# One kernel for window attention and a four-expert attention layer: on-chip places given out by a table, two raw weights kept in one tile, and a new issue order

## The chip, the core and the metric

The kernel runs on one core of a Trainium2 chip. The core has five engines with an instruction queue each: TensorE (PE in the profile: matrix products and transposes), VectorE (DVE), ScalarE (ACT), GpSimd (POOL) and SyncE (SP, which here only issues transfers; ScalarE issues a few as well). Inputs and outputs lie in HBM, operands in SBUF (128 partitions), and results of TensorE in PSUM, which has eight banks of 2 KB per partition. The metric is the time of one execution on the device in microseconds, lower is better; the time of a kernel is the median of its runs.

## The reference, cut to what matters

Eight batches with eight heads of 64 columns and 576 positions. Stage 1 is attention in which a query sees itself and the 63 keys before it. Its result x goes through stage 2, a full causal attention for each of four experts, of which each position uses the two with the largest gate logits.

```python
def _attn_ref(q, k, v):                       # q, k, v: (8, 8, 576, 64)
    scores = scale * np.matmul(q, k.transpose(0, 1, 3, 2))
    mask = (rel >= 0) & (rel < window)        # rel = query - key, window = 64
    attn = softmax(np.where(mask, scores, -1e9))
    return np.matmul(attn, v)
def _moe_ref(x, w_gate, wq, wk, wv, wo):      # x: (8, 576, 512), 4 experts of 64 columns
    logits = x @ w_gate                       # the two largest give the weights w
    for e in range(E):
        q, k, v = x @ wq[e], x @ wk[e], x @ wv[e]
        a = softmax(np.where(causal, -1e9, scale * (q @ k.transpose(0, 2, 1))))
        ye = a @ v @ wo[e]
        out += w[..., e] * ye                 # where e is one of the position's two
    return out
```

## The kernel before, in words

**Two stages on one core.** Two heads form a pair and lie side by side on the 128 partitions; a batch has four pairs (`NP`). Stage 1 is cut into 36 units, each of eight tiles of 64 queries for two heads. Unit u goes through these steps, and the names are those of the rows below: `s1_qk(u)` computes 16 products of queries and keys into two PSUM banks (`s<-k,q`; the fourth pair's inputs lie in a buffer called `st`); ScalarE and VectorE bring them to SBUF as `sm` (VectorE by COPY_PREDICATED, which takes the own block of keys under the mask `own`); VectorE reduces maxima and sums (TENSOR_REDUCE, RECIPROCAL), GpSimd subtracts and scales, ScalarE takes the exponential; `s1_t(u)` transposes `sm` on TensorE (`t<-ident,sm`), ScalarE copies the result into `ft`, and VectorE (for the first nine units) or GpSimd makes the masked `pt` of it; `s1_av(u)` multiplies by the values (`o<-pt,v`). The result x is kept as a high part `xh` and the remainder `xl`.

**Stage 2** takes x with weights that are also split into two parts each (`wkhi`, `wklo`, and so on for q, v, o), so that each product is three matmuls (`three`). `split_weights(i)` does the split: ScalarE copies the raw weight into the high part, VectorE computes the low part by one SCALAR_TENSOR_TENSOR. The weight `wv` carries the four gate columns as well: 260 columns per chunk, of which 256 come from the tensor wv and four from w_gate, by two loads, two copies and two subtractions. Products: `v2ps` (values and gate logits, 12 matmuls for 128 positions), `kps` and `qps` (keys and queries), scores `s<-kt,qt`, softmax (VectorE's `p<-s,causal`, ScalarE's exponential, GpSimd's scaling), transposes of the probabilities by VectorE and transfers, `o<-pt,v` with the expert values, and `ops`, the output product, which is copied to `out` and stored by SP (the very last store by ScalarE).

**Order.** The class `Plan` records every instruction in a list in place of issuing it; a TensorE block (`nc.block`) is one entry. `Plan.issue` then issues the entries in the order of a table of numbers, `LIST` (2769 entries before). So the order on each engine's queue is that table, and semaphores make up the rest. All instructions have the line of the call in `issue`: L203 in the kernel before, L216 after. `warm(k)` is a block of products of `ident` with itself, whose result nobody reads.

**Places.** All PSUM tiles have the tag "s" with `bufs=8`: eight banks given out in rotation in the order in which the code allocates. In SBUF, `sm` rotates over three places of 2 KB, `ft` has one, `out` two (in the last batch some of `out` are in the places of `sm`). A tile that takes a place waits until the last reader of the tile before it is done; for an `out` that reader is the store.

Of the kernel before, what the change touches and what calls it, by code (L numbers as in the profile page):

```python
# [165 lines left out]
)  # L166
TAIL = 2
WARM = 6
BPOS = 0.05
SJOIN = 1  # L170
PARTS = ((0, 5), (5, 9))
# [47 lines left out]
def window_attention_moe_attention(ctx: ExitStack, tc: tile.TileContext, qT, kT, vW,  # L219
# [209 lines left out]
    def s1_av(u):  # L429
# [3 lines left out]
        with nc.block("a"):  # L433
            for i, (x, j, p, b) in enumerate(tiles(u)):
# [5 lines left out]
                if b == BLK - 1 and later(p):  # L440
                    freed.append(p)
# [527 lines left out]
```

## Time and profile before

| | |
|---|---|
| median of three runs | 412.88 us (412.17, 412.88, 413.45) |
| the profiled execution: own time, span | 413.24 us, 411.5 us |
| TensorE busy | 398.9 us, 97% of the span |
| VectorE busy | 310.7 us, 75% |
| GpSimd busy | 276.7 us, 67% |
| ScalarE busy | 260.5 us, 63% |
| chain that ended last | TensorE 87%, VectorE 8%, GpSimd 2% of the span |

The span runs from the first to the last instruction that the profiler saw; the execution's own time has 1.7 us around it. Busy shares are means over the whole span, and a stretch of some microseconds can look quite different from them. Times in rows are microseconds from the start of the span. In a row of the timeline the second number is how long the group lasts, from the start of its first to the end of its last instruction; instructions on VectorE and TensorE overlap a little, so start to start is what the queue takes.

### The profile page before, as it was taken

To read this page: it belongs to the slowest core of one execution; us is meant where nothing else is said; L and a number is where in the kernel's file an instruction comes from. 1 tells how busy PE (TensorE), PEld (TensorE's weight loads), DVE (VectorE), ACT (ScalarE), POOL (GpSimd) and SP (SyncE) were. 2 spreads that over 40 slices of the span, in tenths; PEclk is the share of its full clock that TensorE was granted. 3 is DMA by queue.
4 is the path that set the end of the run, shared out by engine and by line. 5 is a ranking of instruction groups with operands and counts; after the bars stand their busy time and mean duration, and the time that the engine had idled before them with its cause. 6 is when DMAs were issued, how large, how long until landed. Compare 5 with 4: busy or idle time off the path is not lost.

```text
span 411.5 us, 14007 instructions
## 1 busy us (share of the span) xinstructions
PE 398.9 (97%) x5308; PEld 358.9 (87%) x5308; DVE 310.7 (75%) x996; ACT 260.5 (63%) x865; POOL 276.7 (67%) x471
## 2 busy tenths in 40 slices
PE   7689999999999999999999999999999999999996
PEld 7479889999988989898989898988988999898875
DVE  3799998889695878879786876969887768445742
ACT  2666657685748485674858567486856676447852
POOL 3868887977797876887786966877768671504420
PEclk9899999999999999999999999999999999999999
DMA  7987346376867475368776669487657613453113
GB/s 240 349 310 268 111 144 231 78 208 181 239 223 203 135 182 217 106 172 267 193 248 143 205 147 308 130 211 197 176 130 222 151 60 80 131 134 103 53 53 127
DMA packets 33363, 72.69 MB, mean 177 GB/s; under 512 B 6160, under 2 KB 10256, under 8 KB 33296
## 3 DMA queue, kind: packets, MB, share of 16 engines
q1 hardware_dynamic: 32640, 71.14, 58.2%
q8 instruction: 42, 0.69, 0.7%
q10 hardware_dynamic: 656, 0.66, 0.5%
q14 instruction: 25, 0.20, 0.2%
HBM read 39.85 MB, written 9.44 MB: 120 GB/s over the span
## 4 chain that ended last, share of the span: by engine, by line
PE 87%; DVE 8%; POOL 2%; ACT 1%; issue 1%; ACTq 0%; POOLq 0%
PE o L203 18%; PE s L203 17%; PE ops L203 12%; PE v2ps L203 12%; PE kps L203 12%; PE qps L203 11%; PE t L203 4%; DVE pt L203 2%; DVE st L203 2%; DVE sm L203 1%; POOL sm L203 1%; PE warm L203 1%; DVE xl L203 1%; ACT sm L203 0%; DVE wklo L203 0%
## 5 line engine op out<-in xcount | busy, mean ns | idle before, releaser
L203 POOL TENSOR_SCALAR p<-p,r,g 128x448 f32<-128x448 f32 (+4 forms) x135 | 84.0, 636 | 29.5 <-DVE r L203 23.8
L203 POOL TENSOR_TENSOR sm<-sm,st 128x512 f32<-128x512 f32 x72 | 76.9, 1070 | 30.1 <-DVE st L203 20.0
L203 POOL TENSOR_SCALAR_AFFINE_SELECT pt<-ft 64x512 f32<-64x512 f32 x126 | 84.2, 668 | 17.5 <-ACT ft L203 8.4
L203 ACT ACTIVATE p<-p,r 128x192 f32<-128x192 f32 (+3 forms) x135 | 78.7, 588 | 16.9 <-DVE r L203 16.7
L203 PE MATMUL o<-pt,v 128*64 128x64 f32 (+2 forms) x1776 | 80.8, 249 | 1.8 <-DVE pt L203 1.2
L203 PEld LDWEIGHTS o<-pt,v 128*64 128x64 f32 x1776 | 68.2, 138 | 15.0 <-issue 3.2
L203 DVE STREAM_TRANSPOSE st<-p 128x128 f32<-128x128 f32 (+5 forms) x126 | 59.9, 515 | 5.7 <-POOL p L203 5.5
L203 DVE CUSTOM_DVE_ANT_0 p<-s,causal 128x320 f32<-128x320 f32 (+2 forms) x120 | 54.3, 483 | 7.8 <-PE s L203 7.3
L203 DVE TENSOR_REDUCE st<-sm 128x8 f32<-128x512 f32 x72 | 48.4, 679 | 7.0 <-ACT sm L203 6.1
L203 PE MATMUL s<-kt,qt 64*128 64x320 f32 (+3 forms) x480 | 43.3, 318 | 0.0
L203 DVE COPY_PREDICATED sm<-own,s 128x256 f32<-128x256 uint8 x72 | 29.3, 442 | 12.9 <-ACT sm L203 7.7
L203 PE MATMUL kps<-xh,wklo 128*128 128x256 f32 (+1 forms) x128 | 37.7, 295 | 1.2 <-DVE wklo L203 1.2
L203 PE MATMUL kps<-xh,wkhi 128*128 128x256 f32 (+1 forms) x128 | 38.7, 302 | 0.0
L203 PE MATMUL qps<-xh,wqhi 128*128 128x320 f32 (+1 forms) x128 | 38.4, 300 | 0.0
L203 PE MATMUL v2ps<-wvhi,xh 128*128 128x260 f32 x128 | 37.7, 294 | 0.2 <-DVE xl L203 0.2
L203 PE MATMUL s<-k,q 64*64 64x128 f32 (+1 forms) x1116 | 37.8, 275 | 0.1
L203 PE MATMUL qps<-xl,wqhi 128*128 128x320 f32 (+1 forms) x128 | 37.6, 294 | 0.0
L203 PE MATMUL kps<-xl,wkhi 128*128 128x256 f32 (+1 forms) x128 | 37.6, 294 | 0.0
L203 PE MATMUL qps<-xh,wqlo 128*128 128x320 f32 (+1 forms) x128 | 37.6, 294 | 0.0
L203 PEld LDWEIGHTS s<-kt,qt 64*128 64x128 f32 x480 | 35.0, 186 | 2.8 <-issue 0.7
L203 PE MATMUL v2ps<-wvhi,xl 128*128 128x260 f32 x128 | 36.2, 283 | 0.0
L203 PE MATMUL v2ps<-wvlo,xh 128*128 128x260 f32 x128 | 36.2, 283 | 0.0
(124 smaller groups left out, 921.6 us busy)
## 6 DMA issues: line engine op xcount, KB each, us to landing
v<-in_vW_dram SPq DMA_DIRECT2D x28, 576.0 KB, 5.2
pt<-st SPq DMA_DIRECT2D x112, 116.0 KB, 2.3
pt<-st SPq DMA_DIRECT2D x112, 80.0 KB, 2.1
out_dram<-out SPq DMA_DIRECT2D x32, 256.0 KB, 2.5
k<-in_kT_dram SPq DMA_DIRECT2D x28, 288.0 KB, 5.0
q<-in_qT_dram SPq DMA_DIRECT2D x28, 288.0 KB, 5.2
v<-in_vW_dram SPq DMA_DIRECT2D x3, 320.0 KB, 5.9
out_dram<-out SPq DMA_DIRECT2D x7, 128.0 KB, 2.5
```

Source lines behind the costliest of these rows:

```text
L203: call(*args, **kw)
```

## The change

1. The order table `LIST` is another one (2787 entries).
2. PSUM: eight tags of one bank each in place of the rotation; a string of 502 digits, `BANKS`, says which bank each tile takes, in the order of allocation.
3. SBUF: `sm`, `ft` and `out` share seven places of 2 KB (six before); a string of 108 digits, `SLOTS`, says which place each takes.
4. The raw wv and the raw gate weights go into one tile of four rows of 260 columns: the load of wv writes pieces of 256 columns, the load of w_gate pieces of four columns, and `split_weights` does one copy and one subtraction of 128x1040 in place of two of each.
5. `warm` is one matmul and there are 16 of them (six of two before).
6. `s1_qk` and `s1_av` of the units 0 to 3 are one block per pair in place of one per unit, so that the table can place them apart.
7. The `ops` bank is always allocated in full.

```diff
 LIST = (
-    1, 3, 2, 0, 7, 5, 6, 4, 16, 20, 18, 14, 15, 17, 9, 21, 19, 69, 29, 279, 46, 67, 48, 34, 35, 41, 44, 39, 42, 45,
...
+BANKS = (
+    "6737251201400112015230245536711342361037417672062047276356434472370430716515051730015260454245214522"
...
+SLOTS = (
+    "1601445624340310615206524305161165564345202460254161303524524520624136403622425165300534456123641053"
...
-WARM = 6
+WARM = 16
...
-    psum = ctx.enter_context(tc.tile_pool(name="psum", bufs=2, space=PSUM))
+    psum = ctx.enter_context(tc.tile_pool(name="psum", bufs=1, space=PSUM))
+    numbers = iter(BANKS)
+
+    places = iter(SLOTS)
+
+    def bank(shape, name):
+        return psum.tile(shape, F32, tag="s" + next(numbers, "0"), name=name)
+
+    def slot2k(shape, name):
+        return work.tile(shape, F32, tag="slot" + next(places, "0"), bufs=1, name=name)
...
-        t = (PT2[:, 0:1024], PT2[:, 1040:2064], PT2[:, 2064:3088], V2[1].rearrange("r j e c -> r (j e c)"))[i]
+        t = (PT2[:, 0:1040], PT2[:, 1040:2064], PT2[:, 2064:3088], V2[1].rearrange("r j e c -> r (j e c)"))[i]
         name, src, n, _ = WEIGHTS[i]
-        raw = raws[name] = t[:, :1024].rearrange("r (c n) -> r c n", n=src.shape[2])
-        nc.sync.dma_start(raw, src)
+        w = src.shape[2]
+        raw = raws[name] = t[:, :n].rearrange("r (c n) -> r c n", c=src.shape[1])
+        nc.sync.dma_start(raw[:, :, 0:w], src)
         if name == "v":
-            raws["g"] = PT2[:, 3088:3104].rearrange("r (c n) -> r c n", c=4)
-            nc.sync.dma_start(raws["g"], wg)
+            nc.sync.dma_start(raw[:, :, w:], wg)
...
-        at = 0
-        for raw in (raws.pop(x) for x in (name, "g")[:1 + int(name == "v")]):
-            to = slice(at, at + raw.shape[2])
-            nc.scalar.activation(hi[:, :, to], raw, AF.Copy, scale=scale)
-            nc.vector.scalar_tensor_tensor(lo[:, :, to], raw, scale, hi[:, :, to], op0=OP.mult, op1=OP.subtract)
-            at = raw.shape[2]
+        raw = raws.pop(name)
+        nc.scalar.activation(hi, raw, AF.Copy, scale=scale)
+        nc.vector.scalar_tensor_tensor(lo, raw, scale, hi, op0=OP.mult, op1=OP.subtract)
...
+    def parts(u):
+        t = list(tiles(u))
+        return [[x for x in t if x[2] == p] for p in sorted({x[2] for x in t})] if u < 4 else [t]
...
-        banks = [psum.tile([128, 4, 128], F32, tag="s", bufs=8, name=f"s1_{u}_{x}") for x in range(2)]
-        with nc.block("s"):
-            for x, j, p, b in tiles(u):
+        banks = [bank([128, 4, 128], f"s1_{u}_{x}") for x in range(2)]
+        for group in parts(u):
+            with nc.block("s"):
+                for x, j, p, b in group:
...
-        sm = work.tile([128, 512], F32, tag="sm1", bufs=3, name=f"sm1_{u}")
+        sm = slot2k([128, 512], f"sm1_{u}")
...
-        f = work.tile([128, 4, 128], F32, tag="ft", bufs=1, name=f"ft_{u}")[:, :m]
+        f = slot2k([128, 4, 128], f"ft_{u}")[:, :m]
...
         with nc.block("z"):
-            for i in range(2):
-                nc.tensor.matmul(ps[:, 0:128], lhsT=ident, rhs=ident, start=True, stop=True)
+            nc.tensor.matmul(ps[:, 0:128], lhsT=ident, rhs=ident, start=True, stop=True)
...
-        tag, bufs = ("out", 2) if b < NB - 1 or j % 2 else ("sm1", 3)
-        t = work.tile([128, DM], F32, tag=tag, bufs=bufs, name=f"out_{b}_{j}")
+        t = slot2k([128, DM], f"out_{b}_{j}")
```

The order is shown at three places. Numbers behind a name tell tiles apart, and they differ between the two kernels.

The first place is the beginning of SP's queue, the loads. Before, the first rows are:

```order
L203 DMA q_75<-in_qT_dram 128x256
L203 DMA q_73<-in_qT_dram 128x256
L203 DMA st_69<-in_qT_dram 128x256
L203 DMA q_77<-in_qT_dram 128x256
L203 DMA q_75<-in_qT_dram 128x320
L203 DMA st_69<-in_qT_dram 128x320
```

After the change they are:

```order
L216 DMA pt_70<-in_wv_dram 128x4x256
L216 DMA q_75<-in_qT_dram 128x256
L216 DMA q_73<-in_qT_dram 128x256
L216 DMA st_69<-in_qT_dram 128x256
L216 DMA q_75<-in_qT_dram 128x320
L216 DMA q_77<-in_qT_dram 128x256
```

The load of wv has moved from row 16 to row 1, and the first half of the third pair's queries (q_77) from row 4 to row 6. The first halves of the keys are on ScalarE's queue in both kernels. Each load signals on one of eight counters in turn, so the load in row 6 first waits for the load of the counter's row before, which ScalarE's four loads included is wv's.

The second place is the beginning of TensorE's queue. Before:

```order
L203 MATMUL warm_102<-ident 128x128 x2
L203 MATMUL warm_105<-ident 128x128 x2
L203 MATMUL warm_100<-ident 128x128 x2
L203 MATMUL warm_103<-ident 128x128 x2
L203 MATMUL s_0_0_106<-k_74,q_73 64x64 x2
L203 MATMUL s_0_1_107<-k_74,q_73 64x128 x2
```

After the change the queue begins with the scores of unit 0, and from row 31 on, when those of the units 0 to 3 are nearly done, it reads:

```order
L216 MATMUL s_3_0_143<-k_78,q_77 64x128 x2
L216 MATMUL warm_106<-ident 128x128
L216 MATMUL s_3_1_144<-st_69 64x128 x2
L216 MATMUL warm_108<-ident 128x128
L216 MATMUL warm_107<-ident 128x128
L216 MATMUL warm_102<-ident 128x128
L216 MATMUL warm_110<-ident 128x128
L216 MATMUL t_0_122<-ident,sm_0_118 128x128 x4
```

Eight dummies stood ahead of the first scores and none does now; the scores of the units 2 and 3 stand ahead of the first transposes, where before only those of unit 2 did. The 16 dummies are spread over the rows 32 to 132.

The third place is where the scores of stage 2 set in, before on TensorE from row 244 on:

```order
L203 MATMUL s_0_0_1_0_245<-kt_0_217,qt_88 128x448
L203 MATMUL s_0_0_1_1_246<-kt_0_217,qt_88 128x448
L203 MATMUL o_7_205<-pt_7_195,v_152 64x64 x14
L203 MATMUL o_7_205<-pt_7_195,v_179 64x64 x2
L203 MATMUL o_8_213<-pt_8_209,v_179 64x64 x16
...
L203 MATMUL v2ps_3_212<-wvhi,xh_118 128x260
L203 MATMUL v2ps_3_212<-wvlo,xh_118 128x260
```

After the change, from row 285 on:

```order
L216 MATMUL s_0_0_3_0_259<-kt_0_227,qt_88 128x256
L216 MATMUL s_0_0_3_1_260<-kt_0_227,qt_88 128x256
L216 MATMUL s_0_0_1_0_255<-kf_0_226,qf_94 64x64 x2
L216 MATMUL o_7_215<-pt_7_205,v_162 64x64 x14
L216 MATMUL o_7_215<-pt_7_205,v_189 64x64 x2
L216 MATMUL o_8_223<-pt_8_219,v_189 64x64 x16
```

The product v2ps_3 (12 matmuls) and the two score groups s_0_0_2 and s_0_0_3 (six matmuls each) stand ahead of o_7 and o_8 now; they stood behind them. VectorE's queue at the same place was, from row 98 on:

```order
L203 RECIPROCAL st_9_230<-st_9_230 128x8
L203 TENSOR_REDUCE st_10_234<-sm_10_233 128x8
L203 ISA p_1_68,r_0_0_251<-s_0_0_1_1_246,causal 128x448
L203 ISA r_0_0_251 128x1
L203 RECIPROCAL st_10_234<-st_10_234 128x8
L203 TENSOR_TENSOR xl_166<-o_6_191,xh_165 128x512
```

And it is, from row 99 on:

```order
L216 TENSOR_REDUCE st_10_244<-sm_10_243 128x8
L216 TENSOR_TENSOR pt_8_219<-t_8_221,tri 64x4x128 x2
L216 ISA p_1_68,m_0_0_262<-s_0_0_2_0_257,causal 128x320
L216 ISA m_0_0_262 128x1
L216 ISA p_0_67,r_0_0_261<-s_0_0_0_0_253,causal 128x192
L216 ISA r_0_0_261 128x1
L216 ISA p_0_67,r_0_0_261<-s_0_0_0_0_253,causal 128x320
```

The 448-wide row, a reduction, a reciprocal and the subtraction for o_6 have moved behind this place; two 320-wide rows and a 192-wide one stand here now, and behind them TensorE's o_7 may take its bank. Four rows for the gates (batch 0) have come ahead of it as well, at VectorE's rows 93 to 96.

## Rows read from the trace of the kernel before

**Rows 1.** Stretches: length, busy time (instructions) by engine, clock, DMA share, GB/s.

```profile
7.92:25.83 17.91, 12.44 (x240) 9.99 (x232) 15.74 (x30) 11.06 (x29) 12.93 (x18) 0.90 1.01 359
25.83:58.80 32.97, 32.17 (x544) 29.10 (x544) 32.33 (x70) 20.81 (x60) 27.07 (x38) 1.00 0.57 196
60.00:400.00 340.00, 339.83 (x4395) 307.16 (x4394) 257.51 (x883) 223.64 (x765) 232.62 (x396) 1.00 0.58 167
395.00:411.50 16.50, 12.62 (x103) 10.37 (x101) 4.72 (x13) 5.22 (x12) 0.00 (x0) 0.97 0.30 105
```

**Rows 2.** What TensorE waited for: total us, times, longest.

```profile
PE t L203 <- POOL sm L203: 3.1, 4, 2.5
...
PE kps L203 <- DVE wklo L203: 1.2, 1, 1.2
...
PE v2ps L203 <- DVE xl L203: 0.2, 1, 0.2
```

**Rows 3.** Timeline of TensorE: start, length, group.

```profile
5.91 2.11 PE L203 MATMUL s<-k,q 64*64 64x64 f32 x42
...
50.85 1.15 PE L203 MATMUL o<-pt,v 128*64 128x64 f32 x32
...
52.35 0.37 PE L203 MATMUL v2ps<-wvhi,xh 128*128 128x260 f32 x1
...
53.99 1.64 PE L203 MATMUL s<-kt,qt 64*128 64x192 f32 x18
```

**Rows 4.** Timeline of VectorE from 57.5 us on.

```profile
57.51 0.62 DVE L203 CUSTOM_DVE_ANT_0 p<-s,causal 128x448 f32<-128x448 f32 x1
...
58.06 0.20 DVE L203 RECIPROCAL st<-st 128x8 f32<-128x8 f32 x1
58.17 0.64 DVE L203 TENSOR_TENSOR xl<-o,xh 128x512 fp32r<-128x512 f32 x1
58.73 0.48 DVE L203 CUSTOM_DVE_ANT_0 p<-s,causal 128x320 f32<-128x320 f32 x1
...
59.13 0.69 DVE L203 TENSOR_TENSOR xl<-o,xh 128x512 fp32r<-128x512 f32 x1
59.74 0.35 DVE L203 CUSTOM_DVE_ANT_0 p<-s,causal 128x192 f32<-128x192 f32 x1
...
61.98 0.17 DVE L203 TENSOR_REDUCE gs<-logits 128x4 f32<-128x16 f32 x1
62.06 0.56 DVE L203 TENSOR_TENSOR g<-logits 128x64 f32<-128x64 f32 x1
...
62.63 0.21 DVE L203 TENSOR_TENSOR g<-logits 128x64 f32<-128x64 f32 x1
62.77 0.44 DVE L203 COPY_PREDICATED sm<-own,s 128x256 f32<-128x256 uint8 x1
```

**Rows 5.** Groups of VectorE, 7.9 to 58.8 us: busy, mean ns, idle before.

```profile
L203 DVE TENSOR_REDUCE st<-sm 128x8 f32<-128x512 f32 x22 | 14.8, 679 | 1.0 <-ACT sm L203 0.7
...
L203 DVE COPY_PREDICATED sm<-own,s 128x256 f32<-128x256 uint8 x22 | 8.9, 438 | 3.8 <-PE s L203 2.9 <-ACT sm L203 0.8
...
L203 DVE SCALAR_TENSOR_TENSOR wvlo<-pt,wvhi 128x16 fp32r<-128x16 f32 x1 | 0.2, 161 | 0.0
```

**Rows 6.** Loads before 30 us: issues, KB each, median us to landing.

```profile
pt<-in_wv_dram SPq DMA_DIRECT2D x1, 512.0 KB, 7.3
...
q<-in_qT_dram SPq DMA_DIRECT2D x3, 128.0 KB, 2.8
k<-in_kT_dram ACTq DMA_DIRECT2D x3, 128.0 KB, 3.0
```

**Rows 7.** The last copies of `out`, ScalarE's and VectorE's timeline.

```profile
404.89 0.60 ACT L203 ACTIVATE out<-ops 128x512 f32<-128x512 f32 x1 [0.66 <-PE ops L203]
...
407.31 0.42 DVE L203 COPY out<-ops 128x256 f32<-128x256 f32 x1 [0.94 <-PE ops L203]
```

**Rows 8.** Stores of the output, from the page's part on transfers.

```profile
out_dram<-out SPq DMA_DIRECT2D x32, 256.0 KB, 2.5
```

More of the change, by code (lines that the diff above doesn't have):

```diff
@@ L29 @@
 LIST = (
[136 rows of a table removed]
[137 rows of a table added]
+)
+BANKS = (
+    "6737251201400112015230245536711342361037417672062047276356434472370430716515051730015260454245214522"
+    "4411365366203330245601205102142570761442120165126551324561743017726337024071423424653022340142035315"
+    "0351762065314176410252677564774603553066252107034633763121510241741320260452410361255046773175523430"
+    "1245700643360460564254716011204725413673523106770314430413714563724165051656266471256324421737303035"
+    "2672201557416531440267721033571763147257231650445615302426410364035027427315426025054436502314316023"
+    "45"
+)
+SLOTS = (
+    "1601445624340310615206524305161165564345202460254161303524524520624136403622425165300534456123641053"
+    "24560152"
 )
 TAIL = 2
-WARM = 6
+WARM = 16
 BPOS = 0.05
@@ L397, in s1_t @@
         t = PT1[u] = work.tile([128, 4, 2, 128], F32, tag="pt1", bufs=2, name=f"pt1_{u}")[:, :m]
-        f = work.tile([128, 4, 128], F32, tag="ft", bufs=1, name=f"ft_{u}")[:, :m]
+        f = slot2k([128, 4, 128], f"ft_{u}")[:, :m]
         if early:
-            ps = psum.tile([128, 4, 128], F32, tag="s", bufs=8, name=f"t1_{u}")[:, :m]
+            ps = bank([128, 4, 128], f"t1_{u}")[:, :m]
             with nc.block("t"):
@@ L405, in s1_t @@
         else:
-            banks = [psum.tile([128, 8, 64], F32, tag="s", bufs=8, name=f"t1_{u}_{o}")[:, :m] for o in range(2)]
+            banks = [bank([128, 8, 64], f"t1_{u}_{o}")[:, :m] for o in range(2)]
             with nc.block("y"):
@@ L431, in s1_av @@
         size, w, start = SIZES[u], SIZES[u] // 2, STARTS[u]
-        o = psum.tile([128, 8, 64], F32, tag="s", bufs=8, name=f"o1_{u}")
-        with nc.block("a"):
-            for i, (x, j, p, b) in enumerate(tiles(u)):
-                for h in range(2):
-                    c = 64 * (h ^ x)
-                    k = x * w + j
-                    nc.tensor.matmul(o[64 * h:64 * h + 64, i], lhsT=pairs[p][2][h, b],
-                                     rhs=t[:, k // 2, k % 2, c:c + 64], start=True, stop=True)
-                if b == BLK - 1 and later(p):
-                    freed.append(p)
+        o = bank([128, 8, 64], f"o1_{u}")
+        for group in parts(u):
+            with nc.block("a"):
+                for x, j, p, b in group:
+                    i = 2 * j + x
+                    for h in range(2):
+                        c = 64 * (h ^ x)
+                        k = x * w + j
+                        nc.tensor.matmul(o[64 * h:64 * h + 64, i], lhsT=pairs[p][2][h, b],
+                                         rhs=t[:, k // 2, k % 2, c:c + 64], start=True, stop=True)
+                    if b == BLK - 1 and later(p):
+                        freed.append(p)
         i = 0
@@ L540, in warm @@
     def warm(k):
-        ps = psum.tile([128, 512], F32, tag="s", bufs=8, name=f"warm_{k}")
+        ps = bank([128, 512], f"warm_{k}")
         with nc.block("z"):
-            for i in range(2):
-                nc.tensor.matmul(ps[:, 0:128], lhsT=ident, rhs=ident, start=True, stop=True)
+            nc.tensor.matmul(ps[:, 0:128], lhsT=ident, rhs=ident, start=True, stop=True)
     def s2_v(b, j):
-        ps = psum.tile([128, 512], F32, tag="s", bufs=8, name=f"v2ps_{b}_{j}")
+        ps = bank([128, 512], f"v2ps_{b}_{j}")
         with nc.block("VW"[j // 4]):
@@ L604, in proj @@
         c0, n = HALVES[b > 0][half]
-        ps = psum.tile([128, 512], F32, tag="s", bufs=8, name=f"{name}ps_{b}_{pr}_{half}")
+        ps = bank([128, 512], f"{name}ps_{b}_{pr}_{half}")
         w = slice(128 * pr, 128 * pr + 128)
@@ L643, in s2_mm @@
     def s2_mm(b, pr, k):
-        banks = SB[b, pr, k] = [psum.tile([128, 512], F32, tag="s", bufs=8, name=f"s2_{b}_{pr}_{k}_{e}")
+        banks = SB[b, pr, k] = [bank([128, 512], f"s2_{b}_{pr}_{k}_{e}")
                                 for e in range(2)]
@@ L725, in s2_tp @@
             s0, w, m = group[0][0], group[0][1].shape[1], len(group)
-            ps = psum.tile([128, 512], F32, tag="s", bufs=8, name=f"t2_{b}_{pr}_{part}_{k}")
+            ps = bank([128, 512], f"t2_{b}_{pr}_{part}_{k}")
             with nc.block("TU"[part]):
@@ L780, in s2_av_mm @@
         n = 64 * (b1 - b0)
-        o = OB[b, pr, part] = psum.tile([128, 512], F32, tag="s", bufs=8, name=f"o2_{b}_{pr}_{part}")
+        o = OB[b, pr, part] = bank([128, 512], f"o2_{b}_{pr}_{part}")
         with nc.block("AB"[part]):
@@ L809, in s2_o @@
         end = b == NB - 1 and j == 4
-        banks = [psum.tile([128, DM // (1 + end)], F32, tag="s", bufs=8, name=f"ops_{b}_{j}_{i}") for i in range(1 + end)]
+        banks = [bank([128, DM], f"ops_{b}_{j}_{i}")[:, 0:DM // (1 + end)] for i in range(1 + end)]
         for letter, prs in (("O", (0, 1)),) if b < NB - 1 else (("o", (0,)), ("O", (1,))):
```

12 lines of the change are left out of this document (6 added, 6 removed), and 272 rows, old and new, of the table LIST.

## The prediction

> **What bounds the kernel now.** I read the stretches first, then what TensorE waits for, then the timeline of the two engines that matter. From 60 to 400 us TensorE is busy for 339.83 of 340.00 us, and VectorE for 257.51 [rows 1]: there TensorE's own work is the limit, and the view of its waits is empty for that stretch. All waits of TensorE that the trace names lie earlier: 3.1 us of the transposes for GpSimd's part of the softmax (2.5 us in one piece), 1.2 us of kps for the low part of wk, and 0.2 us of v2ps for VectorE's xl [rows 2]. The last of these begins v2ps_3, at about 58.8 us. From 25.83 to 58.80 us VectorE is busy for 32.33 of 32.97 us [rows 1], so in that stretch VectorE sets the pace and TensorE's waits show how far it is behind. From 7.92 to 25.83 us VectorE is busy for 15.74 of 17.91 us [rows 1]: 2.17 us lost, in a stretch in which it has as much to do as it can take. The work on TensorE at the end (from 395 us on) is without a gap until the last matmul, 12.62 us busy [rows 1], and behind that come a copy and a store.
>
> So the time is: the moment at which TensorE passes the last point where it waits for VectorE, plus TensorE's work that is left at that point, plus copy and store. A change in the order can make the first two smaller and hardly the rest.
>
> **TensorE's work after the start.** The dense part has the same products, transposes and shapes after as before; only their order differs, and the number of switches between tile shapes along TensorE's queue, counted in the two orders from the first 64-row transposes on, is 138 before and 137 after. I put it at nothing: no other work hides it, and one switch more or less would show in full (the first matmul of v2ps lasts 0.37 us and all twelve 1.64 [rows 3], so a switch is worth a tenth or two).
>
> **The last wait.** Before, it is that of v2ps_3, for which VectorE must have subtracted for o_6. After, the point that matches is o_7, whose bank comes free behind VectorE's 320-wide row of s_0_0_0. Ahead of that point TensorE has more behind it than before: v2ps_3, 1.64 us by its twelve matmuls (52.35 to 53.99 [rows 3]), and the twelve score matmuls of s_0_0_2 and s_0_0_3, 12/18 of 1.64 = 1.09 us [rows 3]; less o_7 and o_8, which come later now, 2 x 1.15 = 2.30 us by a unit of 32 matmuls [rows 3]. That is 0.43 us of work done earlier.
>
> VectorE, for its part, must do less ahead of that point. Gone from there: the 448-wide row (57.51 to 58.06: 0.55), the reciprocal (0.11), the subtraction for o_6 (59.13 to 59.74 for one of that shape: 0.61) [rows 4], a reduction (679 ns against the subtraction's 0.69, so 0.61 start to start too [rows 4, 5]), and the separate subtraction of the gate columns (161 ns [rows 5]); together 2.04 us. Added: two 320-wide rows of 0.40 (58.73 to 59.13), one 192-wide of 0.35 [rows 4], and the four gate rows. Those take 0.79 us before (61.98 to 62.77), but one of them, 0.56 us, has the shape of the one that takes 0.21 [rows 4]; without that stall they are 0.44. I take 0.44, since the second row of the shape is free of it, and keep 0.79 as the other end. Sum 1.59, net -0.45 us (-0.10 at the other end).
>
> If VectorE's queue stays full up to that point, the two add up: -0.43 - 0.45 = **-0.88 us** (-0.53 at the other end).
>
> **The start.** Three things move. First, the load of wv (512 KB) goes ahead of all queries on SP's queue. Transfers move 359 GB/s in the stretch from 7.92 on with all engines busy [rows 1], and 512 KB take 1.46 us at that rate. The first query loads land 2.8 us after their issue and the keys on ScalarE's queue 3.0 us [rows 6]; these keys are issued alongside and suffer less than the queries behind wv. The delay of VectorE's first COPY_PREDICATED, at 7.92 us in that row of the stretches, is between 0 and 1.46 us; I take the middle, +0.7, since neither queue is plainly ahead. The third pair's queries wait for the landing of wv as well, 7.3 us in the crowd before [rows 6]; they are wanted only for unit 1, for which VectorE has 1.6 us of work on unit 0 as cover (two COPY_PREDICATED of 0.44 and a reduction of 0.68 [rows 5]). If that cover is gone, unit 1 is late next, and it costs up to the same 1.46.
>
> The Trainium skill, page "DMA: Bandwidth & Descriptors", section "Issuing engines are not separate DMA queues", says that transfers started by the scalar, sync or gpsimd engine end up on the same 16 DMA engines and interleave there. By that rule the keys on ScalarE's queue have no way around wv, and the delay would be 1.46 in place of 0.7. The trace agrees as far as it goes: 2.8 and 3.0 us for loads of one size from the two queues [rows 6].
>
> Second, the scores of the units 2 and 3 stand ahead of the first transposes, for which TensorE waited 2.5 us [rows 2]. Before, unit 3's came behind them. VectorE then has COPY_PREDICATED and reductions to do where it stood waiting for ScalarE's part of unit 0 and 1: 0.8 us of its idle time before COPY_PREDICATED and 1.0 us before reductions [rows 5] (the 2.9 us that the first of these rows shows for scores are the wait for the first ones, up to 7.92). Between 0 and 1.8 us come back; I take 1.0, the larger part of it, because five COPY_PREDICATED and three reductions move up, more than the stalls are long, but each unit's softmax still has to go through ScalarE and GpSimd. Third, the 8 dummies ahead of the first scores are gone and 16 lie in later waits. Before, the first 42 small score matmuls took 2.11 us from 5.91 on [rows 3], 50 ns each; they were paced by their loads, and the same holds after. The dummies lie in waits for VectorE and cost nothing as long as VectorE sets the pace; where that cover is gone, the four more cost some 0.55 us, an estimate by the nearest row, twelve matmuls in 1.64 us [rows 3]. Net of the start: +0.7 - 1.0 = **-0.3 us** (-1.8 to +1.46).
>
> One 1040-wide copy on ScalarE and one subtraction on VectorE in place of two each: the subtraction is counted above, and ScalarE is not full anywhere in this stretch.
>
> **The end.** Before, TensorE ends with two 256-wide products, whose copies are VectorE's 256-wide (0.42 us) and ScalarE's; after, it ends with a 512-wide one, copied by ScalarE, 0.60 us [rows 7]. Stores take 2.5 us from issue to landing [rows 8] either way. **+0.2 us** (0 to +0.4).
>
> **Sum**: -0.88 - 0.3 + 0.2 = -0.98 us against the profiled execution's 413.24, so 412.26. That execution lies 0.36 us above the median of the runs shown (412.88), which makes the forecast **411.9**. Something like 0.3% (1.24 us) is what a measurement of this kernel can tell from no change, so the forecast is at the edge of that.
>
> **Rivals.**
>
> *The start gives back all of its stalls and the loads cost nothing* (1.8 us back, +0 for wv): -0.88 - 1.8 + 0.2 = -2.5 us, 410.4. For it: VectorE has the work. Against it: the 512 KB have to move at some time, and the engines for transfers are full from 7.92 to 25.83 us [rows 1].
>
> *The change does not do what it says at the start* (wv costs 0.7 us, no stall comes back): -0.88 + 0.7 + 0.2 = 0, 412.9. For it: the stalls in ScalarE's part of the softmax are latencies of a chain and not a lack of work. This is where the skill's rule leads as well: with 1.46 for wv and 0.8 back it gives the same time.
>
> *Slower: copies wait for stores.* `sm`, `ft` and `out` now share seven places. Where an `sm` or `ft` takes the place of an `out`, the copy by ScalarE or VectorE waits until the store has landed, 2.5 us after its issue [rows 8]; before, only `out` followed `out`. Behind such a copy stands ScalarE's queue, behind that the PSUM bank which the copy would have freed, and behind that TensorE, which has 0.17 us of slack in 340 [rows 1]. One place given out too early in one batch costs up to 2.5 us: 411.9 + 2.5 = 414.4; it decides from 1.0 us on in all, which takes the whole gain. For it: such places exist (in the recorded order some 30 copies or memsets wait for a transfer's counter). Against it: there are seven places and not six, and a table made by hand or by search can put them far apart.
>
> **How the numbers follow.** The forecast's case has 0.47, and its own range is 411.0 to 412.8 (the ends of the hand-over and of the start's two halves). The first rival has 0.17, the second 0.16, the slower one 0.16, and 0.04 are left for what I don't see. The range that leaves out no more than two in ten goes from the first rival's 410.2 to 414.1, short of the slower one. Faster by more than 0.3% is below 411.64: 0.17 from the first rival and half of the forecast's case, 0.40 in all. Slower by more than 0.3% is above 414.12: 0.16. The rest, 0.44, lies within.
>
> **What would show it.** VectorE's first COPY_PREDICATED after the change begins at 8.6 us (0.7 later), and by 26 us VectorE has lost about 1.2 us in place of 2.2. TensorE enters its unbroken stretch behind the wait of o_7, with the 340 us from 60 to 400 again free of waits. The last store is issued about 1 us earlier. I am wrong if TensorE shows waits for ScalarE's or VectorE's copies after 60 us (the slower rival), if VectorE's first row comes at 9.4 us or later (wv), if its idle time before 26 us is again 2 us (the second rival), or if TensorE's busy time in the dense part differs by more than half a microsecond, which nothing above allows for.

## The result, and the profile after

The changed kernel takes 418.61 us (median of four runs, 417.71 to 418.75) where the kernel before takes 413.16 us (four runs, 412.17 to 414.08): 1.0128 times as long, 95% interval 1.0099 to 1.0156. It is slower by 5.5 us, and the forecast was 411.9. The span of the profiled execution is 416.0 us in place of 411.5, 4.5 us more.

First the stretches of the changed kernel, as in [rows 1] (length, then busy time of TensorE, its weight loads, VectorE, ScalarE and GpSimd, the clock, the DMA share and GB/s):

```profile
25.83:58.80 32.97, 31.63 (x467) 28.73 (x467) 32.41 (x65) 20.06 (x59) 25.31 (x36) 1.00 0.61 205
60.00:400.00 340.00, 335.25 (x4418) 305.83 (x4419) 252.74 (x875) 220.76 (x761) 231.89 (x396) 1.00 0.57 165
395.00:416.00 21.00, 17.35 (x156) 13.83 (x154) 6.49 (x18) 7.69 (x18) 1.33 (x2) 1.00 0.34 120
```

The second line answers at once where the time is: from 60 to 400 us TensorE stands for 4.75 us, where it stood for 0.17 us before [rows 1]. What it waits for (us in total, times, longest), over the whole span:

```profile
PE s L216 <- DMA q<-in_qT_dram: 8.5, 2, 6.9
PE o L216 <- DMA pt<-st: 3.9, 5, 1.0
PE o L216 <- DVE r L216: 0.5, 1, 0.5
```

The first line is the start, the second is new: the products `o<-pt,v` with the expert values wait for the *moves*, the transfers `pt<-st` which carry the transposed probabilities to other partitions. Each of 14 groups of them is 16 transfers, all issued by SP. The view names the moves for 3.9 us, but in TensorE's timeline all 4.75 us stand directly ahead of the first product that reads a group's moved probabilities, in eight of the 14 groups. TensorE's timeline at three of its waits after the start:

```profile
58.48 1.24 PE L216 MATMUL s<-kt,qt 64*128 64x448 f32 x11 [0.20 <-DVE pt L216]
...
131.84 4.83 PE L216 MATMUL o<-pt,v 128*64 128x256 f32 x108 [1.00 <-DMA pt<-st]
...
227.86 4.83 PE L216 MATMUL o<-pt,v 128*64 128x256 f32 x108 [1.03 <-DMA pt<-st]
```

And the chain of waits that leads to the second of them (start, length, what), its last pieces:

```profile
128.64 0.59 SPq L216
129.23 0.04 issue
129.28 2.11 DMA pt<-st
131.39 0.46 issue
131.84 1.16 PE o L216 x18
```

Each move takes 0.59 us on SP's queue and 0.04 us to the next; 16 of them are 10 us. The last lands 2.11 us after its issue begins, and TensorE follows. The same group in SP's timeline, in the changed kernel:

```profile
118.75 0.35 SPq L216 DMA_DIRECT2D out_dram<-out  x1
119.15 10.72 SPq L216 DMA_DIRECT2D pt<-st  x15
129.91 0.58 SPq L216 DMA_DIRECT2D v<-in_vW_dram  x1
```

and in the kernel before:

```profile
116.72 4.60 SPq L203 DMA_DIRECT2D pt<-st  x7
121.41 0.53 SPq L203 DMA_DIRECT2D out_dram<-out  x1
121.98 6.23 SPq L203 DMA_DIRECT2D pt<-st  x9
```

VectorE's last transpose of this group begins at almost the same moment in both:

```profile
118.57 0.26 DVE L203 STREAM_TRANSPOSE st<-p 128x128 f32<-128x128 f32 x1
```

```profile
118.42 0.30 DVE L216 STREAM_TRANSPOSE st<-p 128x128 f32<-128x128 f32 x1
```

The first fence is of before, the second of the changed kernel. But the issues of the moves end at 128.21 us before and at 129.87 after, where only one of the 16 is out ahead of the last transpose: the store of `out` that comes second on SP's queue begins at 118.75, when ScalarE's copy for it has just ended (118.12 and 0.60 us), and the other 15 moves stand behind it. TensorE's timeline at these products, before and after:

```profile
133.46 2.80 PE L203 MATMUL o<-pt,v 128*64 128x64 f32 x58
```

```profile
130.38 0.46 PE L216 MATMUL t<-ident,sm 64*128 64x64 f32 x8
```

Before, behind two products v2ps, this row begins with products of stage 1, and the first one that reads moved probabilities starts at some 134.4. After, the transposes are TensorE's last work ahead of it and end at 130.84. Before, the moves had some 4.5 us of reserve there, after none is left. Taking this for all 14 groups from the landing of the last move to TensorE's first use: 0.3 to 4.6 us before, with twelve groups above 2 us; 0.1 to 2.0 us after, with twelve below 0.8 us, where 0.1 to 0.5 us is what passes between a landing and a start that waited for it. On the mean the reserve falls from 2.8 to 0.6 us. A part of that lies on SP's queue: from the first issue of a group to the end of its last it takes 11.2 us on the mean before and 12.4 after, with 5 other transfers between the moves of all groups before and 16 after.

### The profile page after: what moved, and what is told of

Same layout as the page of the kernel before. It is cut to its first block, busy times and chain, and to the rows that moved or that the text cites. A ratio compares the mean times of both kernels' runs of the same rounds, so it can differ in the third digit from the quotient of the medians.

```text
span 416.0 us, 14047 instructions
## 1 busy us (share of the span) xinstructions
PE 397.6 (96%) x5316; PEld 360.6 (87%) x5316; DVE 306.8 (74%) x995; ACT 258.5 (62%) x864; POOL 274.9 (66%) x471
## 3 DMA queue, kind: packets, MB, share of 16 engines
q1 hardware_dynamic: 33408, 71.14, 57.5%
## 4 chain that ended last, share of the span: by engine, by line
PE 66%; SPq 12%; DVE 11%; DMA 7%; issue 3%; ACT 0%; ACTq 0%; DVEq 0%
PE o L216 15%; SPq L216 12%; PE s L216 11%; PE ops L216 10%; PE qps L216 9%; PE v2ps L216 9%; PE kps L216 8%; DVE st L216 4%; PE t L216 3%; DMA pt<-st 3%; DVE pt L216 2%; DMA v<-in_vW_dram 1%; DMA st<-in_kT_dram 1%; DVE sm L216 1%; DMA q<-in_qT_dram 1%
## 5 line engine op out<-in xcount | busy, mean ns | idle before, releaser
L216 POOL TENSOR_TENSOR sm<-sm,st 128x512 f32<-128x512 f32 x72 | 74.7, 1044 | 23.9 <-DVE st L216 13.8
L216 PEld LDWEIGHTS o<-pt,v 128*64 128x64 f32 x1776 | 70.6, 138 | 16.3 <-issue 4.6
L216 ACT ACTIVATE p<-p,r 128x320 f32<-128x320 f32 (+4 forms) x135 | 77.8, 580 | 9.8 <-DVE r L216 9.8
L216 DVE STREAM_TRANSPOSE st<-p 128x128 f32<-128x128 f32 (+5 forms) x126 | 61.4, 516 | 11.7 <-DMA pt<-st 9.2
L216 DVE CUSTOM_DVE_ANT_0 p<-s,causal 128x320 f32<-128x320 f32 (+2 forms) x120 | 53.7, 484 | 11.6 <-PE s L216 11.2
L216 PE MATMUL s<-kt,qt 64*128 64x320 f32 (+3 forms) x480 | 45.1, 320 | 0.3 <-DVE pt L216 0.2
L216 PEld LDWEIGHTS s<-k,q 64*64 64x64 f32 x1116 | 32.3, 138 | 10.1 <-issue 8.8
L216 PE MATMUL kps<-xh,wkhi 128*128 128x320 f32 (+1 forms) x128 | 38.7, 302 | 0.5 <-DVE sm L216 0.4
L216 PE MATMUL kps<-xh,wklo 128*128 128x320 f32 (+1 forms) x128 | 37.6, 294 | 0.0
L216 PE MATMUL kps<-xl,wkhi 128*128 128x320 f32 (+1 forms) x128 | 37.6, 294 | 0.0
L216 ACT ACTIVATE sm<-s 128x256 f32<-128x256 f32 (+3 forms) x88 | 25.9, 326 | 17.4 <-PE s L216 16.6
```

The lines of the kernel that those rows point to most:

```text
L216: call(*args, **kw)
```

## Experiments

All were timed in rounds with the kernel before, whose median was 413.08 us beside the first four, 412.46 beside the next four and 412.48 beside the last. In the edits, MOVED takes entries of the order table to the place behind another entry:

```python
for ns, n in MOVED:
    for x in ns:
        LIST.remove(x)
    LIST[LIST.index(n) + 1:LIST.index(n) + 1] = ns
```

A diff is cut to the lines that matter; `...` marks what is left out. The theories: **A**, SP's queue sets when the last move of a group lands, and TensorE's waits are for that landing, with no reserve left in the changed order. **B**, the moves land late because of traffic, or the wait is for something else. **C**, the waits are only the place where a general lateness shows, and something else is just as late.

### Fewer moves, in both kernels

```diff
                 nc.sync.dma_start(PT2[32 * g:32 * g + 32, FS * a:FS * a + m],
                                   ST[32 * a:32 * a + 32, FS * g:FS * g + m])
+                if x == 3 and 2 * b + pr >= 2:
+                    nc.ops[-1] = []
```

On the changed kernel: 

> The changed kernel without the last four of the 16 moves in each group but the first two (those parts of the moved probabilities stay as an earlier group left them). SP's queue is shorter by 4 x 0.63 = 2.5 us in twelve groups, and nothing else changes. Theory A, TensorE's waits in the dense part are for the landing of the last move, which SP's queue sets: all those waits but the 0.35 us of the second group go, 4.4 us, so 414.2 us. Theory C, something else is just as late: 417 us or more.

On the kernel before: 

> The kernel before without the same four moves in the same twelve groups. Theory A: there the products come 2 to 4.6 us after the last landing in all but two groups, so a shorter queue gives nothing: 413 us within 0.5. If moves cost time before as well (by traffic or by SP's queue): 410 us or less.

These two kernels leave out a part of what stage 2 needs, so they are read for their times alone. Measured: the changed kernel without the four moves takes 413.00 us (1.0008 of before, 0.9994 to 1.0023), the kernel before without them 411.62 us (0.9975, 0.9961 to 0.9989). The same edit gives 5.6 us to the one and 0.9 us to the other. They were expected at 414.2 and at 413 within 0.5, and came 1.2 and 1.4 us lower. TensorE's stretch from 60 to 400 us, of the changed kernel and of before, both without the four moves:

```profile
60.00:400.00 340.00, 339.76 (x4451) 308.25 (x4449) 253.87 (x875) 222.30 (x765) 231.77 (x395) 1.00 0.52 150
```

```profile
60.00:400.00 340.00, 339.95 (x4396) 306.97 (x4388) 255.99 (x875) 222.42 (x763) 230.05 (x393) 1.00 0.53 153
```

4.75 us of waits have become 0.24. This carries theory A, and C falls: nothing else is as late as the moves when nothing but them is taken away. The 0.9 us of the kernel before are not seen in its dense part, where 0.17 us of waits have become 0.05. B in its traffic form is not excluded by this pair alone, since the bytes go too. But the moves land about as fast after as before (the last number is the median from issue to landing, the first line before, the second after), and the dense part carries 167 GB/s before [rows 1] and 165 after:

```profile
pt<-st SPq DMA_DIRECT2D x112, 116.0 KB, 2.3
```

```profile
pt<-st SPq DMA_DIRECT2D x112, 116.0 KB, 2.4
```

Whether places on the queue alone are enough is the next pair's part.

### More issues on SP's queue, in the kernel before

```diff
+                if 4 * x + a >= 14:                        # 8 in the second kernel
+                    mine = nc.ops.pop()
+                    k = 4 * x + a + 16 * (2 * b + pr)
+                    nc.sync.dma_start(JUNK[0:1, k:k + 1], wg[0:1, 0, 0:1])
+                    nc.ops.append(nc.ops.pop() + mine)
...
+    JUNK = const.tile([1, 256], F32, name="junk")
```

Two more issues: 

> The kernel before with two more issues on SP's queue in each of the 14 groups of moves (loads of four bytes that nobody reads, ahead of the last two moves), 0.4 us each. The products come 0.3 to 4.6 us after the last landing in the trace of before. Theory A: only the group with 0.3 us of reserve shows it, 413.7 us. If SP's queue as a whole is full, so that loads and stores behind the moves are due as well: 415 us or more.

Eight more issues: 

> The kernel before with eight more issues on SP's queue in each of the 14 groups, ahead of the last eight moves, 3.4 us a group. Theory A: what goes beyond the reserve of each group shows, 15 us by the reserves of the trace, so 428 us; loads and stores that stand behind the moves can add to it. If the moves' landing had cover that the trace does not show: 415 us or less.

Measured: 414.16 us with two (1.0041, 1.0021 to 1.0060) and 427.92 us with eight (1.0353, 1.0314 to 1.0392). A load of four bytes is no traffic; what it costs is its place on SP's queue, 0.43 us each in the trace:

```profile
125.20 0.43 SPq L203 DMA_DIRECT2D junk<-in_wg_dram  x1
125.68 1.14 SPq L203 DMA_DIRECT2D pt<-st  x2
```

The reserves of before, read from its trace, had given 413.7 and 428. Both times came near, but the traces do not show just the waits that were expected. With two, the group with 0.3 us of reserve shows no wait; TensorE's one wait of more than 0.1 us in the dense part is ahead of the products of another group and named for a load, so that this time came near by luck:

```profile
PE o L203 <- DMA v<-in_vW_dram: 0.9, 1, 0.9
```

With eight, TensorE stands for 8.84 us from 60 to 400 us, in the profiled execution (424.14 us, the fastest of the six). 5.3 us of it stand directly ahead of the first product of a group, in seven groups; the rest is elsewhere, 1.4 us of it ahead of products of stage 1 that wait for a load of v. The view names the moves for about a third, its longest lines being

```profile
PE o L203 <- DMA pt<-st: 2.8, 2, 1.7
PE o L203 <- DMA v<-in_vW_dram: 1.4, 1, 1.4
```

So issues ahead of the moves cost little as long as the reserve lasts, and beyond it they cost time, at the moves and at the loads that stand behind them. Places on the queue are enough for that, without bytes. That the whole 15 us go by the reserves of the moves, as the expectation had it, is not shown.

### Four moves twice

```diff
+                if x == 3:
+                    nc.ops[-1] = 2 * nc.ops[-1]
```

> The kernel before with four of the 16 moves of each group issued twice (the same bytes to the same place), which adds 2.5 us to SP's queue in each of the 14 groups. In the trace of before the products start 0.3 to 4.6 us after the last landing. Theory A: only what goes beyond that reserve shows, about 0.4, 0.6, 0.7, 2.6, 1.5 and 0.7 us in seven groups, 6 us in all, so 419 us. If SP's issues did not set the landing, or the reserve were larger than it looks: 413.2 us.

Measured: 532.89 us (1.2920, 1.2874 to 1.2966), 120 us more in place of 6. The dose was another than planned: the group shown above takes 22.1 us from its first issue to the end of its last, in place of 11.5. So the four added issues took 2.7 us each. A second copy waits, by a semaphore of the program, until a move before it has landed: SP's queue waits for moves 56 times, as often as there are added issues, where it did so once in the kernel before.

```profile
SPq L203 <- DMA pt<-st: 98.2, 56, 3.5
```

TensorE stood for 84 us after 60 us, by these two lines and four shorter ones:

```profile
PE o L203 <- DMA pt<-st: 60.2, 11, 7.4
PE o L203 <- issue: 6.9, 1, 6.9
```

The rest of the 120 us goes with the clock: its mean was 0.908 in place of 0.995, and TensorE is busy for 431.6 us with the same 5308 instructions, in place of 398.9.

### The interposed loads and stores behind the moves

```diff
+MOVED = (((725,), 659), ((805,), 830), ((839, 842, 1038), 974), ((1109,), 1175), ((1197,), 1329), ((1483,), 1502),
+         ((1819, 1910, 1787), 1853), ((2079,), 2003), ((2083, 1872), 2187), ((2479,), 2556))
```

> The changed kernel with the loads and stores that stand between the moves of a group (transfers pt<-st, 16 to a group, all on SP's queue) put behind the last move of that group, in ten of the 14 groups; nothing else moves. Theory A: the products o<-pt,v wait for the landing of the last move, which is late because SP's queue takes 0.63 us for each issue, so each interposed issue costs 0.4 to 0.6 us there; of the waits of 0.35, 1.0, 0.74, 1.03, 0.74, 0.24 and 0.51 us about 3.1 us go, and the time is 415.5 us. Theory B, the moves land late because the transfers themselves are slow (traffic) or the wait is for something else: the time stays at 418.6 us within 0.5.

Measured: 445.33 us (1.0757, 1.0720 to 1.0795). Far from both. The moves' waits fall to 0.3 us, as theory A had it, but the transfers that were put off were just as due. TensorE's waits in the dense part:

```profile
PE o L233 <- DMA v<-in_vW_dram: 9.3, 3, 4.6
PE t L233 <- ACT ft L233: 7.1, 1, 7.1
...
PE o L233 <- DMA pt<-st: 0.3, 1, 0.3
```

and two waits of ScalarE and GpSimd for a store that holds the shared place of an `ft` and of an `sm`:

```profile
ACT ft L233 <- DMA out_dram<-out: 7.6, 1, 7.6
POOL sm L233 <- DMA out_dram<-out: 6.9, 1, 6.9
```

Loads of v came up to 4.6 us late, and ScalarE's wait for a store is the one behind TensorE's 7.1 us for `ft`. What stands between the moves in the changed order could not wait until the moves were out.

### Other TensorE work ahead of the products

```diff
+MOVED = (((981,), 835), ((872, 985), 932), ((1290, 1195), 1271), ((1550, 1554), 1663), ((2306,), 2190),
+         ((2226, 2353), 2305), ((2652, 2650, 2663), 2691))
```

> The changed kernel with one to three TensorE blocks that stood behind the products o<-pt,v put ahead of them, in the seven groups that waited most; SP's queue is untouched. Theory A: the moves land when they land, and TensorE now has 1.5 to 2.6 us of other work meanwhile, so the 4.7 us of waits go and the time is 414 us, unless the blocks put ahead wait for operands or banks of their own. Theory C, the waits are only where a general lateness shows, and TensorE waits later for something else instead: 417 us or more.

In this kernel a projection of batch 6 reads the low part of x ahead of the subtraction that writes it, so it is read for its waits alone. Measured: 428.83 us (1.0375, 1.0347 to 1.0403), with 2.5 us of waits for loads of v after 60 us and more for copies. A narrower version with projections whose operands are there:

```diff
+MOVED = (((985,), 932), ((1290,), 1271), ((1607,), 1663), ((2086, 2306), 2190), ((2353,), 2305))
```

> The changed kernel with one TensorE block each put ahead of the products o<-pt,v in five of the groups that wait for moves: a projection whose operands are long there (a product kps, v2ps or qps, about 1.5 us) in four, four pairs of transposes (0.4 us) in one; in the group of 300 us VectorE's subtraction for it goes ahead too. SP's queue is untouched. Theory A, TensorE only comes too early for moves that land when they can: waits of 1.0, 0.4, 1.03, 0.74 and 0.24 us go, 3.4 us together, 415.2 us. Theory C, something else is as late as the moves and takes the wait over: 418 us or more.

Measured: 425.04 us (1.0290, 1.0261 to 1.0318). The waits for moves fall to 1.0 us, and others come in their place:

```profile
PE kps L228 <- ACT ft L228: 2.3, 1, 2.3
...
PE o L228 <- DMA pt<-st: 1.0, 2, 0.8
```

These are PSUM banks: kps is put 5 us earlier (it began at 136.61 us in the changed kernel), behind transposes that end at 131.68. It begins at 134.00, when ScalarE has copied transposes to `ft` in its own turn (133.56 and 0.38 us), and by the bank table that is the bank it takes. Theory C is right in this narrower sense: with the order and the bank table as they are, none of the blocks tried here could be put into the gap for nothing.

### Moves on two queues

```diff
-                nc.sync.dma_start(PT2[32 * g:32 * g + 32, FS * a:FS * a + m],
+                (nc.scalar if x == 3 else nc.sync).dma_start(PT2[32 * g:32 * g + 32, FS * a:FS * a + m],
```

> The changed kernel with the last four of the 16 moves of each group issued by ScalarE in place of SP, at the same places of the order. Theory A: SP's queue is shorter by four times 0.63 us, 2.5 us a group, more than any wait (1.03 us at most), so 414 us; the price is 56 issues on ScalarE, and where ScalarE reaches them before the transposes are done its copies come late and TensorE waits for banks. Theory B (traffic): 418.6 us or more, since the same bytes move.

Measured: 440.21 us (1.0659, 1.0623 to 1.0694). The second queue can run beside the first. In the first group it did, from the same moment on (SP's twelve moves, ScalarE's four), and the group was out after 10.2 us in place of 12.0:

```profile
77.92 10.22 SPq L216 DMA_DIRECT2D pt<-st  x12
```

```profile
77.89 3.92 ACTq L216 DMA_DIRECT2D pt<-st  x4
```

In the next group ScalarE's four came behind SP's last ones, and the first of them so:

```profile
98.55 7.02 SPq L216 DMA_DIRECT2D pt<-st  x11
```

```profile
106.00 0.52 ACTq L216 DMA_DIRECT2D pt<-st  x1
```

ScalarE's timeline has its own work without a gap from 104 us up to there, so the moves came when its queue reached them. In turn, ScalarE's copies stand behind its moves: 15.6 us of ScalarE's waits are for moves. TensorE's waits after 60 us are named for the moves in 0.7 us only, and for loads and stores in 18.1:

```profile
PE o L216 <- DMA out_dram<-out: 8.6, 2, 5.2
PE o L216 <- DMA v<-in_vW_dram: 6.1, 1, 6.1
```

These waits, too, stand ahead of the first products of groups. The transfers of both queues signal on the same eight counters in turn, so a wait for a move can end with a transfer beside it on its counter; which one was late was not tried apart. The expectation named this price, copies that come late, but not its size.

### The start: wv's load, the dummies, the raw tile

```diff
+MOVED = (((12,), 22),)                                     # wv behind wk
```

> The changed kernel with the load of wv moved from the first row of SP's queue to the place behind the load of wk. Theory A on the start: wv's 512 KB ahead of the queries are what delayed VectorE's first COPY_PREDICATED from 7.92 us (before) to 9.33 us (changed), so it comes back to about 8.0 us, and as VectorE sets the pace up to 58 us, 1.0 to 1.3 us of it reach the end: 417.4 us, with the later waits as they are. Rival: the start has cover, since TensorE and VectorE lose it again before 58 us: 418.6 us.

```diff
+IDLE = range(39, 55)                                       # the 16 dummies
...
         for n in LIST:
+            if n in IDLE:
+                continue
```

> The changed kernel without the 16 dummies; nothing else moves. If they lie in TensorE's waits, as the prediction had it: 418.6 us. If they hold up VectorE in the start, where it sets the pace, up to 16 x 0.2 us come back, 416 us or so at the least; if TensorE's clock falls without them, the start gets slower: 420 us.

The last one is part 4 of the change alone, on the kernel before, with its second copy and subtraction doing all 1040 columns:

```diff
...
-            raws["g"] = PT2[:, 3088:3104].rearrange("r (c n) -> r c n", c=4)
-            nc.sync.dma_start(raws["g"], wg)
+            nc.sync.dma_start(raw[:, :, w:], wg)
...
```

> The kernel before with the raw wv and the raw gate weights in one tile (one copy and one subtraction of 128x1040, at the places where those of the gate weights stood); order and places are those of before. By the prediction this is worth 0.16 us on VectorE and nothing else: 413 us within 0.5. If loads in pieces of 1 KB and of 16 bytes cost: 414 us or more.

Measured, wv behind wk: 418.58 us (1.0142, 1.0109 to 1.0175), as the changed kernel. VectorE's first COPY_PREDICATED begins at 6.17 us, 3.2 us earlier, and nothing of it is left by 30 us: the first kps begins at 28.6 us in place of 28.8. VectorE's timeline shows where it went:

```profile
6.17 0.78 DVE L224 COPY_PREDICATED sm<-own,s 128x256 f32<-128x256 uint8 x2 [1.11 <-ACT sm L224]
...
15.41 0.45 DVE L224 COPY_PREDICATED sm<-own,s 128x256 f32<-128x256 uint8 x1 [1.97 <-PE warm L224]
```

With wv later, the loads that follow are later: scores wait 1.0 us for a load of q at 11.8 us, the dummies behind them run late, and VectorE stands for 2.0 us. The transfers move 358 GB/s from 10 to 20 us with all engines busy; the order of the bytes changes who waits, and the sum hardly. The rival was right.

Without the dummies: 421.85 us (1.0218, 1.0175 to 1.0261), 3.2 us slower than the changed kernel's 418.61, with intervals that do not meet; its six runs lie far apart, from 418.65 to 423.86. Two stretches of it, with the mean granted clock in the third last column:

```profile
10.00:20.00 10.00, 6.53 (x135) 5.45 (x135) 8.26 (x20) 5.72 (x18) 8.28 (x10) 0.90 1.00 313
20.00:30.00 10.00, 8.14 (x177) 7.16 (x176) 9.26 (x16) 7.74 (x19) 8.15 (x12) 0.93 0.96 325
```

With the dummies the clock is 1.00 in both stretches. The first kps comes half a microsecond later without them, and the waits after 60 us are 0.9 us longer. So the dummies of the changed kernel do not cost time, and with them the clock stays at 1.00. The profiled execution is one of the faster (419.32); how the rest of the 3.2 us comes about was not followed further.

The raw tile alone: 413.30 us (1.0014, 0.9996 to 1.0033), no difference, as predicted.

## Why the prediction was wrong

The sign was wrong, and one step did most of it.

**TensorE's work after the start, put at nothing.** This is the step that failed. The prediction took the empty view of waits from 60 to 400 us as proof that the order there is worth nothing, and counted products and switches between shapes. Both counts may hold, but a stretch without waits says nothing about its reserves. The order moves TensorE's products against SP's queue, and the reserve of the moves, 2 to 4.6 us in most groups, could have been read from the trace of before: SP's last issue, 2.1 to 2.3 us to landing, and TensorE's first use. After, 4.75 us of waits stand where 0.17 us stood [rows 1]. Taking four moves out of twelve groups takes the waits to 0.24 us and the time to 413.00. The last of the prediction's own signs of being wrong shows it: TensorE's busy time in the dense part differs by 4.58 us, where half a microsecond was allowed.

**The slower rival** had the right side and the wrong mechanism. It held that copies into the seven shared places wait for stores. In the trace after, no copy of ScalarE or VectorE is shown waiting for a store, and that mechanism appears only in the experiment that put stores off by some 10 us. The place to look was SP's queue, but as the transfers' own issue time and not as a store's landing.

**The start.** VectorE's first COPY_PREDICATED begins at 9.33 us, 1.41 later than before (7.92), twice the 0.7 taken and just below the upper end of 1.46. VectorE's timeline after:

```profile
9.33 0.78 DVE L216 COPY_PREDICATED sm<-own,s 128x256 f32<-128x256 uint8 x2 [4.28 <-ACT sm L216]
```

By the sentence of the Trainium skill that the prediction had set aside ("DMA: Bandwidth & Descriptors", "Issuing engines are not separate DMA queues"), the delay was estimated at 1.46. That the net came so near is luck, for two larger shifts make it up. TensorE's beginning, before, after, and after with wv behind wk:

```profile
2.20 3.78 PE L203 MATMUL warm<-ident 128*128 128x128 f32 x16 [2.20 <-POOL ident L203]
```

```profile
6.88 1.56 PE L216 MATMUL s<-k,q 64*64 64x64 f32 x28 [6.88 <-DMA q<-in_qT_dram]
```

```profile
3.72 1.99 PE L224 MATMUL s<-k,q 64*64 64x64 f32 x32 [3.72 <-DMA k<-in_kT_dram]
```

Before, the first scores began at 5.91 us [rows 3], where the dummies ahead of them ended. The prediction took them as paced by their loads, but the first queries and keys had landed by 3.6 us. In the changed order, wv ahead of the queries moves the first scores from 3.72 to 6.88 us and VectorE's first row from 6.17 to 9.33: it costs 3.16 us there, more than twice the upper end. The first load of queries lands 5.2 us after its issue in place of 2.7, and is issued 0.8 us later. ScalarE's second load of keys lands after 4.5 us in place of 3.1, so the keys suffer less, as the prediction had it. That this load is held up at all agrees with the same section of the Trainium skill, by which transfers started by different engines interleave on the same DMA engines. What the dummies' going (with the rest of the order) gave back is the 1.75 us from 7.92 to 6.17, which the prediction put at nothing. No run here shows a delay of 1.46 us by wv.

Of the stalls up to 58 us, 1.8 us before (0.8, 0.7 and 0.3 by VectorE's waits), 1.3 us are left: 0.5 came back, not 1.0. Net +0.9 in place of -0.3. And the experiment with wv behind shows that a later first row is not a later end: all but 0.2 of its 3.16 us are gone by 30 us.

**The last wait.** The point was not o_7. TensorE's last wait of the start is at 58.48 us, in the scores of stage 2, for VectorE's masked copy `pt`; o_7 came later and waited for nothing. The size came out near: TensorE's last matmul ends at 412.35 us, less 4.75 us of waits after 60 us 407.60; before, 407.62 less 0.17, 407.45. Up to the dense part the change costs 0.15 us, and with +0.9 for the start this leaves -0.75 for the hand-over, where -0.88 was forecast. It is a difference of other terms and not measured alone, and whatever else changed up to there is in it: what becomes of the start's +0.9, and the clock. The mean granted clock from 7.92 to 25.83 us, which the prediction left out, was 0.90 before [rows 1] and is 1.00 after. That the difference lies near the forecast shows nothing of the mechanism.

**The end.** Forecast +0.2, measured -0.23: from the end of the last matmul (411.95 and 0.40 us) to the end of the span it takes 3.65 us after and 3.88 before. ScalarE's last two rows before are

```profile
406.96 1.09 ACT L203 ACTIVATE out<-ops 128x512 f32<-128x512 f32 x2 [1.46 <-PE ops L203]
408.08 0.55 ACTq L203 DMA_DIRECT2D out_dram<-out  x1
```

and ScalarE's last copy after, whose store is SP's:

```profile
412.39 0.60 ACT L216 ACTIVATE out<-ops 128x512 f32<-128x512 f32 x1 [1.66 <-DVE out L216]
```

The copy came as forecast: it ends 0.43 us behind the last matmul before (408.05) and 0.64 after (412.99), +0.21. But the store behind it, taken as 2.5 us either way, did not: from the end of the copy to the end of the span it is 3.45 us before and 3.01 after. Before, ScalarE issues it in 0.55 us and it lands 2.6 us after its issue began; after, SP issues it in 0.33 us and it lands after 2.0.

**Dummies and raw tile.** The raw tile was rightly put at nothing. The dummies were not: eight of them held the first scores back before, and the 16 after are worth some 3 us by the run without them.

Sum: +1.41 - 0.5 - 0.75 + 4.58 - 0.23 = +4.5 us, the difference of the spans. The medians differ by 5.5; the profiled execution is the fastest of the four of the changed kernel (417.71).

What stays open: how the lost reserve divides between moves that land later and products that come earlier in each group (1.7 us and some 3.6 us in the one shown; 1.2 us of 2.2 on the mean go with longer queues of moves); and the 1.4 us between the two kernels that leave out four moves in twelve groups. No run here beats the kernel before: the best is that kernel with work left out, 0.9 us faster.

## What to carry to other kernels

Where a stretch has no waits, read its reserves before you call a new order free: for each kind of operand, when it lands and when it is used. A queue of transfers with a fixed price per issue (here 0.63 us, 16 in a row) is an engine like the others, and an order that brings its consumers to the very moment of landing loses in every group what the estimate was short by. In this order transfers, blocks and banks were all due at once: the orders that put entries off or drew them forward around the moves took 425 to 445 us, so the slack would have to be given back where the order is made. And a net that comes out as forecast proves little while its terms are not measured apart: the start's 1.41 us was 3.16 less 1.75.

## What the runs showed of the hardware

An issue on SP's queue takes 0.59 us for a move of 80 or 116 KB between partitions (0.63 us from one to the next), 0.43 us for a load of four bytes and some 0.4 to 0.5 us for a load of 288 KB of keys or queries, so bytes hardly count in it. SP and ScalarE can issue at the same time: twelve moves in 10.22 us and four in 3.92, from 77.9 us on. A load of 512 KB ahead of the queries on SP's queue moved TensorE's first scores by 3.16 us, where its bytes take 1.46 at the 359 GB/s of [rows 1]; the first keys, issued by ScalarE beside it, landed after 2.2 us, and after 2.9 without it. And long waits cost more than their length: with 84 us of waits, of 4 to 7 us for the most part, the mean granted clock was 0.908 and the time grew by 120 us, while the changed kernel's waits after 60 us, 1.03 us at most, left the clock at 1.00.
